# Gated linear attention with an MLP on one core: first two batches loaded one by one, exp(-L) first in chunk 0, constants in two loads, and a new sequence of turns

## The chip, the core and the metric

The kernel runs on one core of a Trainium2 chip. The metric is the device time of one execution in microseconds (us). Before the change three executions took 438.69, 439.83 and 440.66 us; the median is 439.83 us. The profile was taken in a further execution of 438.57 us, whose span (first to last instruction) is 436.8 us; the 1.8 us between the two lie around the span.

## What is computed

```python
def _attn_ref(q, k, v, alpha):            # each (4, 8, 768, 48): batch, head, step, dim
    state = zeros((B, H, D, D))
    for t in range(S):
        state = alpha[:, :, t, :, None] * state + einsum('bhd,bhe->bhde', k[:, :, t], v[:, :, t])
        y[:, :, t] = einsum('bhd,bhde->bhe', q[:, :, t], state)

def _moe_ref(x, g_ln, w_ch1, w_ch2):      # x: (4, 768, 384), the heads of y side by side
    xn = (x - mean(x)) / sqrt(var(x) + 1e-06) * g_ln
    return x + maximum(xn @ w_ch1, 0.0) @ w_ch2      # w_ch1 (384, 1536), w_ch2 (1536, 384)
```

The weights arrive as 64-bit floats, which the kernel reads as pairs of 32-bit words and turns into 32-bit floats itself.

## The kernel before

**Tiles and stages.** The 768 steps are cut into 6 chunks of 128, and each of the 4 batches goes through each chunk, so there are 24 attention blocks. A block (`attention(c, b)`) does the following:

- ScalarE takes the logarithm of alpha (line 278, tile `la`); TensorE sums it over the steps with a triangular matrix (line 284 in chunk 0, line 288 later, tile `lps`, in PSUM). The sum is called L.
- ScalarE computes exp(L) into the SBUF tile `eq` (line 291) and exp(-L) back into the PSUM tile `lps` (line 292).
- VectorE multiplies k by exp(-L) (line 294) and q by exp(L) (line 296) into the tile `qk`.
- One row of `eq` goes to DRAM (line 301, tile `row`) and comes back as columns (line 361, tile `gate`): the decay of the state over the block.
- TensorE transposes `qk` (line 321, tile `tps`), and ScalarE and VectorE copy the result to SBUF (`qT` line 328, `kT` line 326). TensorE multiplies the two (line 337 in chunk 0, line 345 later, tile `aps`), and VectorE copies the causal half (lines 350 and 355, tile `at`).
- TensorE computes the update of the state (line 371, tile `ups`); VectorE multiplies it by the gate in chunk 0 (line 380), and later adds it to the state (line 384), after which GpSimd multiplies by the gate (line 386). TensorE computes the output (line 397 in chunk 0, line 407 later, tile `yps`).
- ScalarE and VectorE normalize the output (lines 414 to 440, tile `xn`), and TensorE transposes it (line 446, tile `xps`) into `xT`.

The MLP of chunk 0 is a plain product (line 476, tile `hps`, and line 488). From chunk 1 on both products are split into blocks that are combined with fewer multiplications (lines 765 and 588), with sums before and after on VectorE, ScalarE and GpSimd.

**Weights.** Twelve pieces of 768 KB are loaded (line 192, tile `ws`, three buffers) and rounded by five VectorE instructions (lines 204, 206, 208, 212, 214) with one of ScalarE (line 210) between the third and the fourth.

**What sets the order.** Every stage is a Python generator that issues some instructions and yields. The string `ORDER` is a list of turns: each letter names a generator, and a letter runs it to its next yield. `a` to `x` are the attention blocks (`a` to `d` are the batches of chunk 0), `A` to `L` the weight pieces, `Y` and `Z` the first product of chunk 0, `M` and `V` the later products, and so on. So `ORDER` fixes the order of the instructions in every engine's queue, SyncE's queue of transfers too. Each queue runs in order, and an instruction that waits holds up all behind it.

**Start.** ScalarE issues the load of the constants (triangle, identity and a second mask: 160 KB, line 163) and of `g_ln` (line 176). SyncE issues four loads of alpha of chunk 0, one for each batch (192 KB each), and then, as the turns come, k and q of two batches at a time (384 KB each, line 128) and v (line 134). Transfers share eight semaphores in turn, so the ninth waits until the first has landed, the tenth until the second, and so on. TensorE runs eight matmuls on zeros (line 231) while the first data come in.

Of the kernel before, what the change touches and what calls it, by code (L numbers as in the profile page):

```python
# [9 lines left out]
FP32 = mybir.dt.float32  # L10
# [3 lines left out]
AFT = mybir.ActivationFunctionType  # L14
# [8 lines left out]


ORDER = (
    "aaaabbaaddaacbbbbccccaaababbbccdddaaabbbbfeaAfffeeeadaaebbfdaaddceadcccceeeehAdd"
    "gdAccaachbeAgbfbbffffghddddbcggghccibceeeaggghaeebbifffggfBdddddfjcifggeeecAeeCB"
    "hccefiifhhhhcBBYYYdjhiffcjcdYiiYjjZffZiiYYDjDCBDflCCZZZDkYZZZlhhlihhgiiigjjjilYY"
    "gjgghEYYlGEZZGZhEZYlmkhkjggjghllYYYCkkkGEZhlFFHkkiiiYOOFFFlYYenZZZmlhjjYfHHggDjj"
    "GlmjjkeZZZZYhhhSJZYnkkkleekkkkiOlZnkiemmllYZZiinmmmnnfmmYIeIfholHPPSSomjjSSSkSSm"  # L30
    "KIIkkjKKpjJJnnknQfflQoojLLngggmLWWWQPPSPPSSPPpoSoEnhmmgghhnXQXXOXppQppiiiXXQQSSS"
    "mmmnliOjjXXXSmmlnniijMSoWWWoMMrXMMXooMMMMMMmnnnMMMMMRMMmMmMMqMppMMMMMppWMqolorrp"
    "lpppQjjpRRRMMMMMMMpprppMqqqrLnooqqppqqWWWoMMMMRmrMtRMoMMMMRMMMMMMMnnnMMOMMOssqqO"
    "tqsqskMoRooqqtttqWWRNNNMMMMMRRqtNMNNNnnnnNMMMMMMMMMMMlllMkkkMMMkRNNlNNMMNBtvmWtt"
    "pMMNtrllmMMMMrkkrNNMMMMMMMMMossXXXMMtrvvrrrqqqrrXXXooXMMMMMMMXXMMMoXMXrooMMMMMoM"
    "MsMIMMMMsMrMvssvMMMMvtruuustMssrrrtsssuqmMttMMMMRMMMMtMMtuurrrrMMrMppMMMMMMMqROR"
    "MRRRMMMMRRROMpMMMpNOONNNnMMnMMMMRRRNMMMMMNNNMNMMwNMNMMMMMMMMMMMNNNvvMNNvppovxMoM"
    "MMMmMsMMMxqqqvtAXXsssXXvvvXMXvXvttMuMMMMMXXsXuMMMMMMMMMMMuMMMMRMMOtuXMMxMMMMttMM"
    "MMwwwwuquusvuuMMMMMwwwwMMMxuRMMRRRxMMMMMwMRMMRMMMMMMxxxxMMMOOxRMwswwwvRwxuxNNswx"
    "xxNNKquMMMvvttsuuxMMsMMMtRRNNNMMMRMMMxqNNxNwxrrMMMCMMMNMMMONMMNssMMMNMMMMMMvvvww"  # L40
    "vNNMMMwwtXXXXxXxxXMLuuXXMMMXXMMMMMMMMMMMMMMMMMMwMOuMMwxOxxMMvXuuwMMRMMMMMMMMMMMw"
    "JJMMwMMMMMMRRRMMMMMuMRMMMMMvxRRRMMMRMMMMXXXXVXXXOMMXXXRMMRNMMMMMVVNNVVVVVVVNXNMV"
    "VVVRVVVVVMVVVVVVVVVVNRRMNNVVVVVVVVVVVVMRRRRMMMMMVVVVONNNNNMMMMMMNVRVVVVVMMMMMMVV"
    "VRRVVVVRNRNVVOMMNNMMMNGNNMMMMMMNNMMOOKMMMMMMMMMMMNNNRMMMMMMNNNOMMMMHNMMNMMMMMNMM"
    "MMMMMMMM"
)

# [2 lines left out]
def kernel(  # L50
# [51 lines left out]
    raw = ctx.enter_context(tc.tile_pool(name="raw", bufs=B // 2))  # L102
# [10 lines left out]
    r = np.arange(P)  # L113
    const_np = np.concatenate([np.triu(np.ones((P, P), np.float32)), np.eye(P, dtype=np.float32),
                               np.tile(np.triu(np.ones((HS, HS), np.float32)), (2, 1))], 1)

    raws = {}

    def load(c, m, names):

        bs = range(2 * m, 2 * m + 2)
        rows = slice(c * P, (c + 1) * P)
        for n, src in (("a", alpha), ("k", k), ("q", q)):
            if n in names:
                t = raw.tile([P, 2, 2, NP, D], FP32, name=f"r{n}", tag="in", bufs=6)
                step = 1 if n == "a" and c == 0 else 2
                for i in range(0, 2, step):
                    nc.sync.dma_start(
                        t[:, i:i + step].rearrange("t b i p d -> t b (i p d)"),
                        src[bs.start + i:bs.start + i + step, rows].rearrange("b t h d -> t b (h d)"))  # L130
                raws.update({(n, c, b): t[:, b - bs.start] for b in bs})
        if "v" in names:
            vn = raw.tile([P, 2, 2, NP, D], FP32, name="vn", tag="vn")
# [3 lines left out]
            if c:  # L137
# [3 lines left out]
                src = v[bs.start:bs.stop, rows].rearrange(  # L141
                    "b (s t) (i p) d -> s i t b (p d)", s=2, i=2)
# [3 lines left out]
            for b in bs:  # L146
                raws["v", c, b] = vn[:, b - bs.start], vx[:, b - bs.start] if c else None

    lone = {}

    def load_one(n):
# [8 lines left out]
                              rows.rearrange("t h d -> t (h d)"))  # L160

    consts = cpool.tile([P, 2 * P + HS], FP32, name="consts")
    nc.scalar.dma_start(consts, nc.inline_tensor(const_np, name="consts").ap())
    tri, ident = consts[:, :P], consts[:, P:2 * P]
    mask, mask_of_halves = tri.bitcast(INT32), consts[:, 2 * P:].bitcast(INT32)
    for m in range(B // 2):
        load(0, m, "a")

    w1 = cpool.tile([P, NJ // 2, NF, 2 * P], FP32, name="w1")
    w2 = cpool.tile([P, NJ, DM], FP32, name="w2")  # L170
# [94 lines left out]
    def attention(c, b):  # L265


        whole, last = c == 0, c + 1 == NCB
        if whole and b % 2 == 0:
            load(0, b // 2, "kq")  # L270
            yield
            load(0, b // 2, "v")
            yield

        qk = qk_of(c, b).rearrange("t n p i c -> t n i p c")[:, :, :, :, :D]
        eq = eq_of(c, b).rearrange("t p i c -> t i p c")[:, :, :, :D]
# [17 lines left out]
        nc.vector.tensor_mul(qk[:, 1], raws.pop(("k", c, b)), lv)  # L294
        yield
        nc.vector.tensor_mul(qk[:, 0], raws.pop(("q", c, b)), eq)  # L296
        ends = slice(P - 1, P) if whole else slice(HS - 1, P, HS)
# [581 lines left out]
```

## Time and profile before

| | |
|---|---|
| median of three executions | 439.83 us (438.69 to 440.66) |
| profiled execution | 438.57 us, span 436.8 us |
| TensorE (PE) busy | 425.2 us, 4760 matmuls |
| VectorE (DVE) busy | 340.0 us, 654 instructions |
| ScalarE (ACT) busy | 202.4 us |
| GpSimd (POOL) busy | 156.0 us |
| granted TensorE clock | full in all slices |
| moved by DMA | 45.53 MB |

In the profile a line such as "L294 DVE TENSOR_TENSOR qk<-rk,lps" is the instruction of line 294 on VectorE that writes tile `qk` from tiles `rk` and `lps`; the brackets behind a row give the idle time of the engine before it and what ended it. PEld is TensorE's loading of weights, which runs beside its matmuls; SPq and ACTq are issues of transfers. Matmuls on 32-bit data show as two rows each, transposes as one. The busy time of TensorE is modelled, so short waits can hide in it; the time between the starts of matmuls shows them.

The trace also records when the last packet of each transfer landed. For the loads at the start these are, in us from the start of the span:

| transfer | KB | issued | landed |
|---|---|---|---|
| alpha, batch 0 | 192 | 0.73 | 3.86 |
| constants | 160 | 0.76 | 4.06 |
| alpha, batch 1 | 192 | 1.19 | 4.54 |
| g_ln | 1.5 | 1.17 | 4.73 |
| alpha, batch 2 | 192 | 1.65 | 5.94 |
| alpha, batch 3 | 192 | 2.12 | 7.68 |
| k, batches 0 and 1 | 384 | 2.59 | 8.73 |
| q, batches 0 and 1 | 384 | 3.07 | 9.77 |
| v, batches 0 and 1 | 384 | 3.87 | 10.83 |
| k, batches 2 and 3 | 384 | 6.28 | 11.85 |
| q, batches 2 and 3 | 384 | 6.71 | 12.89 |

Each transfer is spread over 16 DMA engines. From alpha of batch 3 on, one of the 16 finishes about 1.05 us behind the other fifteen (6.63 against 7.68 us for that transfer): a single packet of it took 1.34 us at 4.59 us, where most take 0.065 us.

### The profile page before, as it was taken

To read this page: it belongs to the slowest core of one execution; us is meant where nothing else is said; L and a number is where in the kernel's file an instruction comes from. 1 tells how busy PE (TensorE), PEld (TensorE's weight loads), DVE (VectorE), ACT (ScalarE), POOL (GpSimd) and SP (SyncE) were. 2 spreads that over 40 slices of the span, in tenths; PEclk is the share of its full clock that TensorE was granted. 3 is DMA by queue.
4 is the path that set the end of the run, shared out by engine and by line. 5 is a ranking of instruction groups with operands and counts; after the bars stand their busy time and mean duration, and the time that the engine had idled before them with its cause. 6 is when DMAs were issued, how large, how long until landed. Compare 5 with 4: busy or idle time off the path is not lost.

```text
span 436.8 us, 11605 instructions
## 1 busy us (share of the span) xinstructions
PE 425.2 (97%) x4760; PEld 379.5 (87%) x4760; DVE 340.0 (78%) x654; ACT 202.4 (46%) x499; POOL 156.0 (36%) x164
## 2 busy tenths in 40 slices
PE   6998999999999999999999999999999999999996
PEld 4887888875678889998789998889998899999996
DVE  3997999898898889957769756678685589786682
ACT  4795656554534546734285141655246442402000
POOL 1011041310015556042854133672026472638213
PEclk9999999999999999999999999999999999999999
DMA  8989877755162085022351013310033000001201
GB/s 271 333 197 331 257 228 222 201 146 147 45 175 72 22 220 165 1 93 74 58 151 50 18 39 126 59 21 2 2 110 108 2 1 2 0 0 56 78 32 55
DMA packets 54973, 45.53 MB, mean 104 GB/s; under 512 B 26204, under 2 KB 51036, under 8 KB 54920
## 3 DMA queue, kind: packets, MB, share of 16 engines
q1 hardware_dynamic: 54376, 44.63, 34.9%
q8 instruction: 37, 0.61, 0.6%
q10 hardware_dynamic: 544, 0.17, 0.2%
q14 instruction: 16, 0.13, 0.1%
HBM read 35.25 MB, written 9.53 MB: 103 GB/s over the span
## 4 chain that ended last, share of the span: by engine, by line
PE 80%; DVE 8%; DMA 6%; ACT 2%; issue 1%; POOL 1%; SPq 1%; POOLq 0%; ACTq 0%
PE ops L588 29%; PE hps L765 29%; PE ops L488 5%; PE yps L407 4%; PE aps L345 3%; PE tps L321 3%; DMA rq<-in_q_dram 3%; PE xps L446 2%; PE ups L371 2%; PE hps L476 2%; DVE w L206 1%; DMA vn<-in_v_dram 1%; DMA gate<-row 1%; DVE ws L212 1%; PE lps L288 1%
## 5 line engine op out<-in xcount | busy, mean ns | idle before, releaser
L604 POOL TENSOR_TENSOR ob<-ob,u 128x192 f32<-128x192 f32 x40 | 24.9, 632 | 81.9 <-DVE ob L601 57.8
L765 PE MATMUL hps<-sum,w 128*128 128x256 f32 x192 | 47.2, 379 | 0.0
L386 POOL TENSOR_TENSOR mid<-mid,gate 112x192 f32<-112x192 f32 x20 | 17.6, 880 | 70.8 <-DVE mid L384 60.0
L765 PEld LDWEIGHTS hps<-sum,w 128*128 128x128 f32 x192 | 35.9, 190 | 4.6
L588 PE MATMUL ops<-w,hT 128*128 128x192 f32 x224 | 39.6, 326 | 0.0
L816 ACT ACTIVATE hT<-hT 128x512 f32<-128x512 f32 x48 | 28.1, 631 | 21.6 <-POOL hT L787 13.2
L588 PEld LDWEIGHTS ops<-w,hT 128*128 128x128 f32 x224 | 37.0, 190 | 0.4
L765 PE MATMUL hps<-xT,w 128*128 128x256 f32 x136 | 34.6, 381 | 0.0
L476 PE MATMUL hps<-xT,w 128*128 128x256 f32 x144 | 32.6, 379 | 1.8 <-DVE qk L294 1.8
L488 PE MATMUL ops<-w,hT 128*128 128x384 f32 x96 | 31.7, 487 | 0.0
L476 PEld LDWEIGHTS hps<-xT,w 128*128 128x128 f32 x144 | 26.7, 190 | 5.3 <-issue 2.0
L598 DVE TENSOR_TENSOR ob<-ops,ob 128x192 f32<-128x192 f32 x50 | 17.1, 351 | 15.9 <-POOL ob L604 8.8
L588 PE MATMUL ops<-ws,sum 128*128 128x192 f32 x160 | 28.8, 326 | 0.0
L488 PEld LDWEIGHTS ops<-w,hT 128*128 128x128 f32 x96 | 17.9, 190 | 11.8 <-ACT qT L328 0.2
L765 PEld LDWEIGHTS hps<-xT,w 128*128 128x128 f32 x136 | 25.3, 190 | 3.3
L588 PEld LDWEIGHTS ops<-ws,sum 128*128 128x128 f32 x160 | 26.3, 190 | 0.0
L386 POOL TENSOR_TENSOR st<-st,gate 112x192 f32<-112x192 f32 x16 | 12.6, 786 | 35.5 <-DVE st L384 35.5
L321 PE MATMUL tps<-consts,qk 128*112 128x128 f32 x176 | 24.2, 275 | 0.0
L588 PE MATMUL ops<-ws,hT 128*128 128x192 f32 x128 | 23.4, 326 | 0.0
L345 PE MATMUL aps<-qT,kT 48*64 48x64 f32 x640 | 23.1, 222 | 0.0
L321 PEld LDWEIGHTS tps<-consts,qk 128*112 128x112 f32 x176 | 19.9, 134 | 3.0 <-DVE qk L296 0.6
L407 PE MATMUL yps<-st,qT 48*64 48x48 f32 x320 | 22.3, 219 | 0.0
(230 smaller groups left out, 1159.3 us busy)
## 6 DMA issues: line engine op xcount, KB each, us to landing
ws<-in_moe_w_ch_dram SPq DMA_DIRECT2D x12, 768.0 KB
vn<-in_v_dram SPq DMA_DIRECT2D x12, 384.0 KB
kept<-x SPq DMA_DIRECT2D x24, 192.0 KB
ob<-kept SPq DMA_DIRECT2D x24, 192.0 KB
out_dram<-ob SPq DMA_DIRECT2D x19, 192.0 KB
ra<-in_alpha_dram SPq DMA_DIRECT2D x16, 192.0 KB
rk<-in_k_dram SPq DMA_DIRECT2D x6, 384.0 KB
rq<-in_q_dram SPq DMA_DIRECT2D x6, 384.0 KB
```

The costliest lines, as they stand in the source:

```text
L321: nc.tensor.transpose(tps[:, p], qk_of(c, b)[:, i, p].rearrange("p a b -> p (a b)")[:, :R], ident)
L345: nc.tensor.matmul(aps[0][halves[1 - i], p, s], kT[rs, p, s], qT[rs, p, s], start=True, stop=True)
L371: nc.tensor.matmul(up[h, p], qk_of(c, b)[ts, 1, p, i, :h.stop - h.start], vn[ts, i, p], start=True, stop=True)
L386: nc.gpsimd.tensor_mul(new, new, by)
L407: nc.tensor.matmul(yps[r][halves[s], i, p], of, by, start=True, stop=True)
L476: nc.tensor.matmul(hps, w1[:, j // 2, f, j % 2 * P:][:, :P], xT_of[0][:, f, bs], start=(f == 0), stop=(f == NF - 1))
L488: nc.tensor.matmul(ops_of[b], hT_of[c][:, j, b], w2[:, j], start=(j == 0), stop=(j == NJ - 1))
L588: nc.tensor.matmul(acc, lhs[:, j], rhs[:, j], start=(j == 0), stop=(j == NT - 1))
L598: nc.vector.tensor_add(x, acc, x)
L604: getattr(nc.gpsimd, f"tensor_{op}")(x, x, y)
L765: nc.tensor.matmul(acc[:, i], w, b, start=True, stop=True)
L816: nc.scalar.activation(out=x, in_=x, func=AFT.Relu)
```

## The change

The loads of chunk 0 for batches 0 and 1 become six transfers of 192 KB in the order alpha, k, q of batch 0, then alpha, k, q of batch 1 (`load_first`). Alpha, k and q of batches 2 and 3 are loaded together, 384 KB each, in the first turn of batch 2, as later chunks do. In chunk 0 ScalarE computes exp(-L) before exp(L), and writes it into the SBUF tile `la` (the logarithms, which are no longer needed) where it wrote to PSUM before. The constants come in two loads: the triangle (64 KB) first, and the identity with the second mask (96 KB) behind `g_ln`. The string `ORDER` is new throughout; its first lines are shown. The number of compute instructions on each engine is unchanged; SyncE and ScalarE issue one transfer more each.

```diff
-    "aaaabbaaddaacbbbbccccaaababbbccdddaaabbbbfeaAfffeeeadaaebbfdaaddceadcccceeeehAdd"
-    "gdAccaachbeAgbfbbffffghddddbcggghccibceeeaggghaeebbifffggfBdddddfjcifggeeecAeeCB"
+    "acaaaaaabbbbbbccaaadaaccbbccddbbdfdaaabeeeffbbaebbbcBdbfaAefccccddddadBgddcccbbb"
+    "ghabbBffBeeeeecccgaaaacchfbggAffddhhddfafgffdffCgabiAAjgggjjeaiiffeeggfhhceieecc"
...
-                step = 1 if n == "a" and c == 0 else 2
-                for i in range(0, 2, step):
-                    nc.sync.dma_start(
-                        t[:, i:i + step].rearrange("t b i p d -> t b (i p d)"),
-                        src[bs.start + i:bs.start + i + step, rows].rearrange("b t h d -> t b (h d)"))
+                nc.sync.dma_start(t.rearrange("t b i p d -> t b (i p d)"),
+                                  src[bs.start:bs.stop, rows].rearrange("b t h d -> t b (h d)"))
...
+    def load_first():
+
+        ts = [(n, src, raw.tile([P, 2, 2, NP, D], FP32, name=f"r{n}", tag="in", bufs=6))
+              for n, src in (("a", alpha), ("k", k), ("q", q))]
+        for b in range(2):
+            for n, src, t in ts:
+                raws[n, 0, b] = t[:, b]
+                nc.sync.dma_start(t[:, b].rearrange("t i p d -> t (i p d)"),
+                                  src[b, :P].rearrange("t h d -> t (h d)"))
...
-    nc.scalar.dma_start(consts, nc.inline_tensor(const_np, name="consts").ap())
+    const_src = nc.inline_tensor(const_np, name="consts").ap()
+    nc.scalar.dma_start(consts[:, :P], const_src[:, :P])
...
-    for m in range(B // 2):
-        load(0, m, "a")
+    load_first()
...
         nc.scalar.dma_start(g_col, g_ln.rearrange("(f p) -> p f", p=P))
+    nc.scalar.dma_start(consts[:, P:], const_src[:, P:])
...
         if whole and b % 2 == 0:
-            load(0, b // 2, "kq")
+            if b:
+                load(0, b // 2, "akq")
...
-        nc.scalar.activation(out=eq, in_=lv, func=AFT.Exp)
-        nc.scalar.activation(out=lv, in_=lv, func=AFT.Exp, scale=-1.0)
+
+        by = la if whole else lv
+        for out, sign in ((eq, 1.0), (by, -1.0))[::-1 if whole else 1]:
+            nc.scalar.activation(out=out, in_=lv, func=AFT.Exp, scale=sign)
         yield
-        nc.vector.tensor_mul(qk[:, 1], raws.pop(("k", c, b)), lv)
+        nc.vector.tensor_mul(qk[:, 1], raws.pop(("k", c, b)), by)
```

More of the change, by code (lines that the diff above doesn't have):

```diff
@@ L25 @@
 ORDER = (
-    "aaaabbaaddaacbbbbccccaaababbbccdddaaabbbbfeaAfffeeeadaaebbfdaaddceadcccceeeehAdd"
-    "gdAccaachbeAgbfbbffffghddddbcggghccibceeeaggghaeebbifffggfBdddddfjcifggeeecAeeCB"
[L28 to L43, printed above, removed]
@@ L44 @@
-    "VRRVVVVRNRNVVOMMNNMMMNGNNMMMMMMNNMMOOKMMMMMMMMMMMNNNRMMMMMMNNNOMMMMHNMMNMMMMMNMM"
+    "acaaaaaabbbbbbccaaadaaccbbccddbbdfdaaabeeeffbbaebbbcBdbfaAefccccddddadBgddcccbbb"
+    "ghabbBffBeeeeecccgaaaacchfbggAffddhhddfafgffdffCgabiAAjgggjjeaiiffeeggfhhceieecc"
+    "cgYffhhhihYddCYeYckjceeedAjiegggkhhhhdCeCBiikiiYddhhffYYDDZZlYYgZZZZhhlEDiiYiiii"
+    "ggEEjjelYYYYYYEHZllCDllHFlZZZkhjiiHihFjjGZggFhFiileeZmlGkhnZYYmllZnGGjCjlOelHelI"
+    "YYmImOOmYYjYYjJkkkkkZZmmmIIKjJhJJKLLmmPPKKPPLPWePooOhjjkknkiiiiiggggkknjmjnoomIW"
@@ new lines @@
+    "mSSnngnnngjjOPhPhhhkQlfSSSSSWWSSZZkkSQQgjjmmppnnkffmmmOfpplnlppZZZZZSfXXXXZXkkkS"
+    "SSSSpopppQQlXXXXXXGmWmnnWlQQWnnMMMMMMoqllQMMmMMllWMMMMMMMMSMqqpppppqqnnpqoooMMMM"
+    "OnMMrrpooooroooiiMMMrRWWllMMMMMMMMMMrMRRRRMMMnnMMMMMMnRnnrtRqqqqMMMWMMMRMMkMRotq"
+    "qMpmoooDpNNlNNRRNloMMMWWMMMNonmMjjMMMMMpkkNNNqMRMNkNNMrrOppMMrMNrMMsMMsrrqkpmmMM"
+    "MMMMomtkNNNppMqMssqMMXjjpjMXFqXXttMMMOMXXXMMrrtrqqrqqsvsMntttrMMMMMMMrrvXXtXXtts"
+    "sMvMMMvuMssMrrOOMMMMMMMMMMMMMMMMRRuRRsssttttMssmvMMMMMMuMMMMMMMMMMMMMMuMMMquMMML"
@@ new lines @@
+    "MmoovMnRRMMttRRRMMMNNNNMMMOttpMMRRMNNNNMMtMMMMMMLqrNNRNoMMNMMMqqquNxvvMMMMMNvNwM"
+    "MMsssvMMMMMuMMMpNrrssswwvvvvvwwooXsXuuMuXwXXXXXMMMMMxuuuvvxuxXXMMMMMMMMMvvMxtMMM"
+    "MMMMXMMMMMMMMMMttMMusRRRMMMRMMMsMMMxxRtRMMOOMMMxxMMruwMMwwwMMMxMMtMMMuuuwwuvRRww"
+    "wrxxxxxxqssMMMsARNRMMMsRONNNxuuNNwwNNNwOrMMMMrRMMMMMvMMMMMMuwNNxttNNMMMMMMMMqXXX"
+    "XNXXXMMMwNMNMMMMMuXXXXMMuMMMMMMMMMMMMMwwwMMMMMOOwMxxRMMMxHMMMMMMMMMMxxvRRMMMMMvv"
+    "MxMMMMMMwRMMMMxMMwMMMMMuxvvRRRREMMMRMMRMRNNNNMMNMMXVXXXXXXVMNMMNMMOMMXXXXMMMMRVV"
@@ L45 @@
+    "VVVVNNNVVVVVVVVVMVVNMMMVMMOMMMNVVOVVVVVVVVVVVVRRVVNVVVVJVBVVVVVVVVMMMRRRMRMNNMOV"
+    "VVVVNMMMMMMMRRVVVVVVMMMMMKORMNNMMONNMMMRRMNNMMMRNNNMMMMMNNNMMMMMMNMMNMMMMMMNNMMM"
     "MMMMMMMM"
```

## The prediction

> **What bounds the kernel now.** The first part of the page gives busy time by engine:
>
> ```profile
> PE 425.2 (97%) x4760; PEld 379.5 (87%) x4760; DVE 340.0 (78%) x654; ACT 202.4 (46%) x499; POOL 156.0 (36%) x164
> ```
>
> TensorE's work doesn't change, so only its idle time can be won. I take it from the time between the starts of matmuls: where each kind's steady pace (in us: 0.109 a transpose, 0.125 L337, 0.063 L397, 0.432 L476 and L765, 0.326 L588) is exceeded, TensorE waits. From the first real matmul on this adds up to 13.7 us: 2.9 before 10.4 us, 2.6 from there to 37.1, 1.95 in one gap there, and 6.2 after 39.3, scattered. Behind the last matmul come some 4 us of sums and stores. So the page's busy time hides waits; a table of stretches (us busy, with counts) shows who is full in the head:
>
> ```profile
> core 0: us, PE busy (x) PEld busy (x) DVE busy (x) ACT busy (x) POOL busy (x), PEclk, DMA share, GB/s
> 4.50:10.40 5.90, 3.38 (x10) 1.14 (x8) 1.16 (x3) 3.11 (x7) 0.00 (x0) 1.00 1.02 348
> 10.40:20.00 9.60, 9.59 (x162) 8.14 (x163) 8.92 (x18) 6.35 (x15) 0.00 (x0) 1.00 1.01 320
> 20.00:30.00 10.00, 10.00 (x225) 8.83 (x223) 9.73 (x17) 9.46 (x28) 1.44 (x2) 1.00 0.93 273
> ```
>
> VectorE does almost nothing before 10.4 us and is then full; the DMA engines are full from the start. The timeline says what VectorE waits for, and how closely its work follows afterwards:
>
> ```profile
> 8.86 0.55 DVE L294 TENSOR_TENSOR qk<-rk,lps 128x384 f32<-128x384 f32 x1 [6.19 <-DMA rk<-in_k_dram]
> 9.79 0.56 DVE L296 TENSOR_TENSOR qk<-rq,eq 128x384 f32<-128x384 f32 x1 [0.38 <-DMA rq<-in_q_dram]
> 10.27 0.55 DVE L294 TENSOR_TENSOR qk<-rk,lps 128x384 f32<-128x384 f32 x1
> 10.73 0.55 DVE L296 TENSOR_TENSOR qk<-rq,eq 128x384 f32<-128x384 f32 x1
> ```
>
> It waits 6.19 us for k, then one product follows the other every 0.47 us. So the head is first DMA-bound, then VectorE-bound, to about 37 us. The table of waits for 26 to 40 us names the next two:
>
> ```profile
> POOL mid L386 <- DMA gate<-row: 2.4, 1, 2.4
> PEld hps L476 <- issue: 2.0, 1, 2.0
> ```
>
> GpSimd waits for a gate column to land (32.8 us). The gap of 1.95 us in TensorE's stream at 37.1 us (inside the first MLP products, L476) has no releaser: "issue". The page's DMA part explains it:
>
> ```profile
> q8 instruction: 37, 0.61, 0.6%
> ```
>
> 37 packets of 16 KB for 2 x 4760 TensorE instructions make one block of 256 instructions each. One such packet ran from 36.75 to 37.94 us, and the gap ended 1.3 us later. The gaps at 54.1 (0.44), 83.5 (0.56) and 215.0 us (1.26) lie at the same place modulo 256 instructions (within 10). So where TensorE runs through a block of small matmuls faster than the next block comes, it stands still.
>
> **The change, part by part.**
>
> *Loads.* The sixteen engines share one stream, so I place the new transfers by bytes in the table of landings: alpha, k and q of batch 0 land at 3.86, 4.54 and 5.94 us, alpha of batch 1 (now fourth) at 7.68, k and q of batch 1 by 8.7, alpha, k and q of batches 2 and 3 at 9.8, 10.8 and 11.85, v at 12.9. The triangle (64 KB of the 160) is there when the whole was, 4.06, or sooner. The extra issues (0.4 to 0.5 us each on SyncE and ScalarE) lie ahead of waits that end last anyway: ScalarE's next instruction waits for alpha until 3.88 us.
>
> *The chain of chunk 0.* L278 at 3.88, matmul at 4.51, its result at 5.40 as now. exp(-L) comes first: ready 5.88, so k of batch 0 is multiplied at 5.9 instead of 8.86. But in TensorE's new queue the sum of batch 1 stands ahead of the transposes of batch 0, and it needs the fourth transfer: logarithm 7.70 to 8.22, matmul 8.27, result 9.16 (0.89 as for batch 0), exp(-L) to 9.65, k of batch 1 at 9.7, q at 10.2. Then ScalarE's queue decides: exp(L) 9.55, the logarithm of batch 2 at 10.0, qT 10.4, the logarithm of batch 3 at 10.9, exp(-L) of batch 2 from 11.4 to 11.9. VectorE: k 11.9, q 12.4, kT 12.9, k 13.5, q 14.0, so the first L350 starts at 14.45 instead of 14.93: **0.5 us earlier**. If the one lagging DMA engine does not lag (alpha at 6.63, the rest 1.05 us earlier) the same steps give 13.35: 1.6 us. So an early start of 3 us shrinks to 0.5 to 1.6.
>
> *exp(-L) into SBUF.* ScalarE's median is 491 ns into SBUF (L291) and 486 into PSUM (L292); VectorE takes 547 ns with the PSUM operand (L294), 552 without (L296). Nothing either way. The Trainium skill ("ScalarE: Activation LUTs", Step-by-step: what each stage is for) says that PSUM is the faster destination for ScalarE, which speaks against this edit; the rows show 5 ns, and four of them would be 0.02 us.
>
> *The sequence.* From L350 on VectorE's queue is nearly the old one for 13 us of work. Then the new sequence puts the first three instructions of the second weight piece (0.58 + 0.99 + 0.48 = 2.05 us, L204, L206, L208) ahead of the L436 that makes `xn` of batch 1, for which TensorE waits (L446). TensorE has almost the same work before that point: 24.3 us instead of 24.7 (four transposes of 0.109 fewer). Before, the two rows stand so:
>
> ```profile
> 30.28 0.47 DVE L436 TENSOR_SCALAR xn<-x,few 128x384 f32<-128x384 f32 x1
> 31.23 0.49 PE L446 MATMUL xps<-consts,xn 128*128 128x128 f32 x3
> ```
>
> After: 30.75 + 2.05 less 0.5 to 1.6 is 31.2 to 32.3, so TensorE has idled 0.5 to 1.5 us more there than before. Second limit: the load of the second weight piece (768 KB, at 1.05 us for 384 KB about 2.1 us) now stands in SyncE's queue ahead of the gate that landed at 32.77:
>
> ```profile
> 32.90 0.51 POOL L386 TENSOR_TENSOR mid<-mid,gate 112x192 f32<-112x192 f32 x1 [2.44 <-DMA gate<-row]
> ```
>
> It lands at 34.9 at worst, GpSimd is done by 35.4, and the L407 that reads the product comes after 27.7 us of TensorE work: 35.5 - 1.05 (its start) - 27.7 = 6.7 us idle, against 5.0 before at that kind of place (33.97 us, 28.0 of work). With DMA gaps taken up (share 0.93), less. I take **+1.2 us** for this stretch (bounds +0.5 and +1.6).
>
> *Instruction blocks.* Counted along the new queue, the block that cost 1.95 us (4.7 us of TensorE work to cover its load) becomes two blocks of 4.0 and 4.45 us. At that time a block took 3.3 us from request to packet, 1.2 to move and 1.1 to act. Against that TensorE now waits for VectorE and the gate part of the time. I take 1.35 us (bounds 0.5 and 2.3): **-0.6**. Later, the old queue has four blocks with 2.0 to 2.6 us of work, and the gaps of 0.56 and 1.26 fall on two of them; the new one has one of 2.8, the rest 3.9 or more. I take **-1.3** (bounds 0 and -2.2). The Trainium skill ("Runtime: NRT & Kernel Launch", Instruction fetch mechanics) states blocks of 16 KiB, 256 instructions, and calls crossing a boundary mostly hidden. The block size agrees with the 37 packets; the trace's 1.95 us is not hidden. By the page both terms would be nothing, and the sum +1.6.
>
> *VectorE's lead later.* Between 60 and 100 us of TensorE work, VectorE's work up to the results that TensorE waits for was 6 to 8 us less than TensorE's own; now it is 2.1 to 3.4 less. VectorE was by then 12 to 15 us behind its count, mostly waiting on others. What cover is left I can't see: **+0.4** (bounds 0 and +1.5).
>
> *The end* is unchanged: the last eleven VectorE and GpSimd instructions stand in the same order.
>
> **Sum:** +1.2 - 0.6 - 1.3 + 0.4 = -0.3 us: 438.57 becomes 438.3. The median shown lies 1.26 above the profiled execution, so 439.5 against 439.83. What a measurement tells from no change is about 0.5%, 2.2 us.
>
> **Rivals.**
>
> 1. *As summed* (no change that can be told): the earlier start is used up by the second weight piece. 439.5; its own bounds add up to -3.15 and +3.45, and 437.6 to 442.0 is its range. This holds the case that the change doesn't do what it says, because TensorE's transposes of batch 0 stand behind batch 1's sum: the first L350 stays at 14.9, and 0.5 is added.
> 2. *Faster:* no DMA engine lags, VectorE gains 1.6 us, and the blocks of instructions come in time: +0.5 - 1.45 - 2.2 + 0.2 = -2.95, so 436.9. For: the four short blocks are gone. Against: the lag came from one packet of 1.34 us among first accesses, and the new order has as many first accesses.
> 3. *Slower, by the late gate:* the place is GpSimd's first L386. From 34.1 us on (VectorE's own limit) each us that the gate lands later is a us of TensorE. For: DMA share 0.93 to 1.0 in this time, 768 KB put ahead. Against: the column is small, and DMA had gaps after 28 us. To lose 2.2 us in all, with the other terms as summed, it must land about 36.6; with VectorE's next sums queued behind it the price is then some 2.5 us: 442.3.
>
> **How the numbers follow.** Chances: as summed 0.45, faster 0.32, slower 0.23; the same stand for within 0.5%, faster and slower. The predicted time is 439.5. The range takes in rival 2 with a bit beyond its sum (436.0) and rival 3 (442.8); outside lie the bounds met all at once.
>
> **What would show it.** First VectorE L294 at 5.9, first L350 at 13.3 to 14.5; the L446 of batch 1 at 31.2 to 32.4; first L386 of GpSimd at 34 to 35.5, waiting for the gate; the first L476 after 29.3 us of work, near 37 (before 36.0 after 29.8); a gap "issue" there of 0.5 to 2.3 us; afterwards gaps at block boundaries of less than 1 us in sum, where there were 2.3. It is wrong if VectorE starts L350 before 13, if the L446 is not late, or if the idle time after 60 us, where I only counted queues, differs by more than 2 us.

## The result, and the profile after

The changed kernel takes 445.91 us (median of 4 runs, 444.87 to 448.08) beside 440.25 for the kernel before: a ratio of 1.0153, 95% interval 1.0107 to 1.0199. Forecast were 439.5 and a range of 436.0 to 442.8, so it is slower than the whole range. A second measurement, beside other experiments (new_again below, 10 runs of 440.0 to 445.56), gave 1.0085 (1.0056 to 1.0114). It is slower in both, by an amount that differs from run to run.

The profiled execution took 448.08 us with a span of 446.3, the slowest of the four. First the page of the kernel after, its part 1 and the row of the granted clock in 40 slices:

```profile
PE 432.0 (97%) x4760; PEld 381.9 (86%) x4760; DVE 341.4 (77%) x654; ACT 203.4 (46%) x499; POOL 153.7 (34%) x164
...
PEclk9999998999999999999999999999999999999999
```

TensorE's busy time rose by 6.8 us at the same 4760 matmuls. Part of that is clock: the seventh slice (67 to 78 us) is below 9. The table of stretches of the kernel after, with the columns of before:

```profile
core 0: us, PE busy (x) PEld busy (x) DVE busy (x) ACT busy (x) POOL busy (x), PEclk, DMA share, GB/s
4.50:10.40 5.90, 4.03 (x16) 2.12 (x16) 2.55 (x5) 3.33 (x8) 0.00 (x0) 1.00 0.96 314
10.40:20.00 9.60, 8.74 (x127) 6.84 (x126) 7.70 (x16) 5.99 (x15) 0.00 (x0) 1.00 1.00 330
20.00:30.00 10.00, 10.00 (x178) 8.05 (x176) 9.86 (x18) 8.47 (x24) 0.95 (x1) 1.00 1.00 305
...
40.00:45.00 5.00, 2.38 (x10) 2.07 (x10) 3.79 (x9) 2.04 (x6) 1.00 (x2) 0.84 1.05 305
70.00:74.00 4.00, 1.55 (x83) 1.37 (x76) 3.02 (x4) 1.37 (x2) 0.22 (x1) 1.00 0.58 176
74.00:78.00 4.00, 4.00 (x16) 3.29 (x15) 2.25 (x4) 3.20 (x10) 0.00 (x0) 0.57 0.66 231
```

VectorE starts sooner (5 instructions by 10.4 us, before 3), as planned. The new sights are two stretches in which TensorE stands still, 40 to 45 and 70 to 74 us, and a lower granted clock that begins behind each standstill (0.84 in the first stretch, 0.57 from 74 to 78 us). The table of waits names what released TensorE in them (who waits, for what; us in total, times, the longest):

```profile
PE tps L332 <- issue: 2.7, 1, 2.7
...
PE yps L418 <- issue: 2.4, 1, 2.4
```

Nothing: "issue", as for the gap at 37 us before the change. Between the starts of the matmuls, less a steady step, these two gaps are 2.87 us (from 39.6) and 2.56 us (from 70.8); gaps below are given so. The single instructions answer to those shown of before (the timeline of the kernel after: start, duration, and in brackets the idle time ahead and what ended it; L305, L361, L447, L457 and L397 are the old L294, L350, L436, L446 and L386):

```profile
6.59 0.56 DVE L305 TENSOR_TENSOR qk<-rk,la 128x384 f32<-128x384 f32 x1 [3.92 <-ACT la L303]
...
14.21 1.93 DVE L361 COPY_PREDICATED at<-consts,aps 128x512 f32<-128x512 int32 x3
...
30.81 1.38 DVE L216 TENSOR_SCALAR ws<-ws 128x768 int32<-128x768 int32 x1
...
30.83 0.95 POOL L431 MEMSET at<- 128x1024 f32 x1 [2.29 <-PE yps L408]
...
32.84 0.47 DVE L447 TENSOR_SCALAR xn<-x,few 128x384 f32<-128x384 f32 x1
...
33.45 0.52 PE L457 MATMUL xps<-consts,xn 128*128 128x128 f32 x3 [0.65 <-DVE xn L447]
...
34.27 0.51 POOL L397 TENSOR_TENSOR mid<-mid,gate 112x192 f32<-112x192 f32 x1 [2.49 <-DVE mid L395]
```

The head gains 0.7 us by 14.2 (forecast 0.5 to 1.6) and loses it by 33: `xn` of batch 1 is 2.6 us later than before, and TensorE now waits for it.

Where the time went, by TensorE's time over its steady pace (idle, and lost to a slow clock), in us of each stretch:

| kernel | 0 to 10 | 10 to 35 | 35 to 60 | 60 to 100 | after | sum |
|---|---|---|---|---|---|---|
| before, profiled at 438.57 | 3.0 | 2.6 | 2.5 | 1.5 | 4.1 | 13.7 |
| after, profiled at 448.08 | 3.2 | 5.0 | 4.5 | 5.4 | 4.2 | 22.3 |
| the same (new_again), profiled at 440.00 | 2.9 | 5.4 | 1.6 | 0.9 | 3.4 | 14.1 |

Two profiles of one program: a loss of 2.4 and 2.8 us more than before between 10 and 35 us is in both, the rest is in one only. The sums are short by some 1 us for the changed kernel: they exceed that of before by 8.6 and 0.4 us, the spans by 9.5 and 1.4.

### The profile page after: what moved, and what is told of

It is laid out like the page before. It is cut to its first block, busy times and chain, and to the rows that moved or that the text cites. A ratio compares the mean times of both kernels' runs of the same rounds, so it can differ in the third digit from the quotient of the medians.

```text
span 446.3 us, 11603 instructions
## 1 busy us (share of the span) xinstructions
PE 432.0 (97%) x4760; PEld 381.9 (86%) x4760; DVE 341.4 (77%) x654; ACT 203.4 (46%) x499; POOL 153.7 (34%) x164
## 4 chain that ended last, share of the span: by engine, by line
PE 82%; DVE 8%; issue 3%; DMA 2%; ACT 2%; POOL 1%; POOLq 0%; SPq 0%; DVEq 0%
PE ops L599 28%; PE hps L776 26%; PE ops L499 7%; PE hps L487 5%; PE yps L418 4%; PE tps L332 3%; PE aps L356 3%; PE xps L457 2%; PE ups L382 2%; DMA ra<-in_alpha_dram 1%; DMA rq<-in_q_dram 1%; DVE w L214 1%; PE lps L239 1%; PE lps L297 1%; DVE more L559 1%
## 5 line engine op out<-in xcount | busy, mean ns | idle before, releaser
L615 POOL TENSOR_TENSOR ob<-ob,u 128x192 f32<-128x192 f32 x40 | 26.6, 674 | 83.6 <-DVE ob L612 61.4
L397 POOL TENSOR_TENSOR mid<-mid,gate 112x192 f32<-112x192 f32 x20 | 14.1, 710 | 64.7 <-DVE mid L395 39.2
L487 PE MATMUL hps<-xT,w 128*128 128x256 f32 x144 | 35.8, 400 | 0.1
L776 PE MATMUL hps<-xT,w 128*128 128x256 f32 x136 | 34.3, 379 | 0.0
L487 PEld LDWEIGHTS hps<-xT,w 128*128 128x128 f32 x144 | 27.8, 200 | 4.4 <-DVE qk L305 0.5
L776 PEld LDWEIGHTS hps<-xT,w 128*128 128x128 f32 x136 | 25.5, 190 | 3.2
L332 PE MATMUL tps<-consts,qk 128*112 128x128 f32 x176 | 25.6, 279 | 0.0
L795 POOL TENSOR_TENSOR hT<-hT,u 128x512 f32<-128x512 f32 x8 | 10.4, 1296 | 43.9 <-DVE u L794 43.9
L418 PEld LDWEIGHTS yps<-st,qT 48*64 48x64 f32 x320 | 20.6, 135 | 5.1 <-issue 4.2
```

Source lines behind the costliest of these rows:

```text
L332: nc.tensor.transpose(tps[:, p], qk_of(c, b)[:, i, p].rearrange("p a b -> p (a b)")[:, :R], ident)
L397: nc.gpsimd.tensor_mul(new, new, by)
L418: nc.tensor.matmul(yps[r][halves[s], i, p], of, by, start=True, stop=True)
L487: nc.tensor.matmul(hps, w1[:, j // 2, f, j % 2 * P:][:, :P], xT_of[0][:, f, bs], start=(f == 0), stop=(f == NF - 1))
L615: getattr(nc.gpsimd, f"tensor_{op}")(x, x, y)
L776: nc.tensor.matmul(acc[:, i], w, b, start=True, stop=True)
```

## The experiments

Theories, by the letters used in the expectations. **A**: TensorE's code comes in blocks of 256 instructions; the fetch of a block queues behind bulk loads, TensorE stalls, and the stall slows the clock. **B**: the new sequence's order on VectorE. **C**: the edits of code in the head. **D** came later: the clock in the first 10 us. Lags below are from where TensorE's count crosses into a block to the start of the next fetch packet; records are missing here and there, so a lag is good to about 1 us. The end of a stall needs no such count: in the nineteen profiles the starts of two matmuls in a row lie over 1 us apart 37 times after 20 us, and 31 of these gaps end 1.2 to 1.6 us after the end of a fetch packet (before the change 37.94 and 39.28 us; after it 41.20 and 42.62, 72.06 and 73.42). The waits table names VectorE, ScalarE or GpSimd for the other six.

### The two halves of the change apart: new_code_old_order, old_code_new_order

The first has the code of after with the old ORDER (its first `c` moved from place 12 to 1):

```
-    "acaaaaaabbbbbbccaaadaaccbb...
+    "acaaabbaaddaabbbbccccaaaba...
```

> The changed kernel's code (loads batch by batch, exp(-L) first and into SBUF, constants in two loads) under the old sequence of turns; one turn, the first of the third attention step, had to move from place 12 to place 1, because the code now issues that step's alpha load there. Theory A (TensorE's instruction blocks are fetched behind bulk loads, and where a block boundary meets a full queue is set by the sequence): the boundaries stand against the loads as before the change, so 440 us, within 1.5 of the kernel before, at a granted clock of 1.0, with no wait without releaser above 2.3 us. Theory B (the new sequence's order on VectorE, the second weight piece ahead of xn of batch 1, costs the time): also about 440. Theory C (the edits of code in the head cost it): 444 to 446, as the changed kernel.

Measured: 443.72 us, ratio 1.0108 (1.0076 to 1.0139). All three missed. In the profile (441.71, the shortest of four) the whole loss lies before 16 us: the first attention product (the old L337) starts at 15.14 us, before 12.37, and from there to 334 us the two run 2.7 to 3.1 us apart. Part of it is the clock, granted at half from 11.44 to 14.85 us: the sixteen transposes that took 2.02 us before the change take 3.40.

```profile
11.81 3.40 PE L332 MATMUL tps<-consts,qk 128*112 128x128 f32 x16
```

```profile
11.40:14.90 3.50, 3.50 (x17) 3.13 (x16) 0.69 (x1) 1.73 (x4) 0.00 (x0) 0.51 0.89 285
```

The second has the code of before with the ORDER of after.

> The code of before (alpha loaded for all batches at the start, exp(L) first, one load of constants) under the new sequence of turns. Theories A and B (the sequence alone): 443 to 447 us, with two waits of TensorE without releaser of over 2 us, near 40 and near 71 us. Theory C (the edits of code): 439 to 441.5, as before.

Measured: 446.88 us, 1.0186 (1.0161 to 1.0211), with gaps of 2.19 us at 42.0, 2.08 at 48.3 and 1.52 at 72.9. The two stretches are as A has them, but the head loses again: first attention product at 15.43, with the clock at half from 8.19 to 15.02 us. So the halves can't be told apart by crossing them: each crossing costs about 3 us in the head, by waits and by a slow clock after them. That each sequence fits the order in which its own code's loads land is likely, but not shown.

### The blocks moved: new_shift128, old_shift160

```
+    def tiny(n):
+        for _ in range(n):
+            nc.tensor.matmul(idle[:32, :1], zero[:, :32], zero[:, :1], start=True, stop=True)
-    for _ in range(8):
+    for _ in range(6):
         nc.tensor.matmul(idle[:, :P], zero, zero, start=True, stop=True)
+    tiny(10)
...
             nc.tensor.matmul(lps[:, :DM], tri, a, start=True, stop=True)
+            if b == 0:
+                tiny(24)
```

> The changed kernel with 128 more TensorE instructions at its start (32 more matmuls of the warm-up, tiny ones of 32 rows by 1 column; 6 instead of 8 full ones), so that every later boundary between blocks of 256 instructions falls 128 instructions earlier in the work; the rest of the program is the same. Theory A: the waits of 2.87 us at 39.6 and 2.56 us at 70.8 go, and the halved clock after each of them, unless new ones come where the shifted boundaries lie close together (near 32 and near 47 us, 4.3 and 4.8 us for a block): 439 to 442 us at a granted clock of 1.0. Theory B or C: 444 to 447, whatever happens to the two waits, since the time lost would then be lost again at the next wait for VectorE. The tiny matmuls themselves may cost up to 1 us at the start.

Measured: 442.83 us, 1.0101 (1.0083 to 1.0119), the profiled run 441.0. The median lies between the two forecasts. Both big stalls are gone; gaps of 1.38 at 37.3 and 0.94 at 44.5 remain. Since in another run of the unaltered kernel they are 0.97 us and nothing (new_again, below), this profile alone doesn't show that the stall follows the count of instructions; the next kernel does.

old_shift160 does the same to the kernel before (12 and 30 tiny ones).

> The kernel before the change with 160 more TensorE instructions at its start (40 more matmuls in the warm-up, tiny ones, 6 full instead of 8), nothing else. Theory A: the boundaries move away from the full stretch of the queue, the wait of 1.95 us at 37 falls to at most 0.6 and that of 1.17 us at 215 goes, so 0.5 to 2.5 us faster than the kernel before, or even with it if the tiny matmuls cost 1 us in the first 10 us. If where the boundaries fall does not matter: the same time as before within 0.5 us plus the cost of the tiny matmuls, the wait at 37 unchanged.

Measured: 443.34 us, 1.0077 (1.0046 to 1.0108), but unevenly spread: three runs at 439.6 to 439.9, seven at 442.6 to 443.9. In the profile (439.88) the gaps at 37 and 215 are gone and new ones of 1.5 at 128.9 and 1.09 at 258.9 are there, where two boundaries now lie 1.8 and 1.9 us apart. The gap near 37 us stands in all six profiles with the old order and boundaries unmoved or nearly so (1.7 to 3.6 us) and in none of the three with moved ones (this kernel, old_fill_shift160, old_fill_shift128): it follows the count of instructions, not the work. The three shorter runs show a mean clock of 0.995 to 0.996, the seven longer ones 0.998 to 1.0; a late start of the full clock would do that (old_order_edits, below), but none of the longer runs was profiled.

### Fewer loads ahead of the fetch: new_split_load, new_late_load

```
             load_one(n - 1)
-            load_one(n)
...
             next(turns[turn], None)
+            if i == 286:
+                load_one(3 * B + 1)
```

> The changed kernel with three of the six 192 KB loads that were issued between 63.3 and 65.9 us (chunk 3, batch 1) put behind the next weight load, at about 71.5 us; nothing else differs. Theory A: the transfers ahead of the block's fetch shrink by 0.58 MB, about 1.6 us of the queue, so the wait of 2.56 us at 70.8 falls to about 1, no halved clock follows it, and the kernel is 2 to 4 us faster than the changed one: 441 to 444. Theory B or C: 444 to 447, no gain.

Measured: 444.81 us, 1.0132 (1.0112 to 1.0153). The wait at 70.9 is 1.51 us instead of 2.56, and no halved clock follows; the one at 40.3 is 2.74. In time no gain is shown (1.0132 against 1.0153 and 1.0085), and since the unaltered kernel has a run with no wait at this place (new_again), the shorter wait proves nothing by itself.

new_late_load moves one `C` of ORDER from place 127 to behind 152.

> The changed kernel with one turn moved: the load of 768 KB that was issued at 32.5 us goes behind the three loads of the next chunk, to about 36.7 us, which is after the point (35.75) where TensorE's queue crosses into a new block. Nothing else differs. Theory A: 0.77 MB, about 2.1 us of transfers, no longer stand ahead of the block's fetch, so the wait of 2.87 us at 39.6 falls to about 1, no halved clock follows it, and the kernel is 1.5 to 3 us faster than the changed one: 442 to 444 on the scale of a kernel before at 440. If the fetch were late for another reason than the loads ahead of it: the wait stays at 2.5 to 3 us and the time at 444 to 446.

Measured: 445.39 us, 1.0157 (1.0103 to 1.0211): no gain. In the profile the stall near 40 did go (0.2 us of "issue" is left in that stretch), but there are gaps of 1.61 us at 48.8 and 2.05 at 74: the moved load may now stand in the way of the next fetch. The profiled run is the longest of four (449.14; the others 444.52 to 445.86): TensorE waited 1.9 us for VectorE's `kT` at 21.6, and the clock was at half from 23.61 to 30.43 us.

### The second weight piece later: new_shift128_late_piece

The kernel is new_shift128; in its ORDER the three `A` at 109, 132, 133 go behind 130, 131, 146.

> As new_shift128, and the second weight piece's three VectorE instructions (2.0 to 3.0 us before xn of batch 1) put behind the xT of that stage, its other two behind the sums of the next state; all before the first hidden product needs the piece. Theory B (the new sequence's VectorE order costs the 2.2 us that TensorE idles more than before the change between 10 and 35 us): xn of batch 1 comes 2 us sooner, TensorE's wait of 0.8 us at 32 goes, and the kernel is 1 to 2.5 us faster than new_shift128. Theory A alone (only the blocks count): within 0.7 us of new_shift128, since the same VectorE work is then late for the next thing.

Measured: 445.21 us, 1.0134 (1.0100 to 1.0169), slower than new_shift128. `xn` is in time, but the piece's ScalarE instruction now stood ahead of a logarithm. Waits and timeline of this kernel:

```profile
PE lps L305 <- ACT la L293: 3.6, 1, 3.6
```

```profile
37.29 0.97 ACT L218 ACTIVATE ws<-ws,small 128x768 int32<-128x768 int32 x1 [3.51 <-DVE ws L216]
38.16 0.51 ACT L293 ACTIVATE la<-ra 128x384 f32<-128x384 f32 x1
```

ScalarE waits 3.51 us for VectorE's L216 with the logarithm queued behind, and TensorE for that. The experiment added a wait and doesn't decide on B; a better placed one follows below.

### The edits without the new sequence: old_order_edits

The diff is the change's, without ORDER, and with alpha of the other two batches still loaded at the start:

```
-    for m in range(B // 2):
-        load(0, m, "a")
+    load_first()
+    load(0, 1, "a")
```

> The kernel before the change, its sequence untouched, with the three edits of the head: the first two batches loaded batch by batch (alpha of the other two behind them, still at the start), exp(-L) first and into SBUF, constants in two loads. new_code_old_order lost 2.8 us in the first 15 us, and there one turn had been moved to place 1. If the edits themselves lose it under the old sequence (its TensorE order asks for the third and fourth batches' alpha early, which now comes later): 2 to 3.5 us slower than before. If the moved turn lost it: within 1 us of before, the first product of VectorE 0.5 us or so sooner.

Measured: 442.82 us, 1.0076 (1.0044 to 1.0108), 3.4 us over the kernel before beside it: the edits lose it without the moved turn. The timeline of TensorE, here and before the change:

```profile
9.22 2.93 PE L294 MATMUL lps<-la,consts 128*128 128x384 f32 x4 [0.35 <-ACT la L288]
11.95 2.92 PE L332 MATMUL tps<-consts,qk 128*112 128x128 f32 x16
```

```profile
9.47 0.91 PE L284 MATMUL lps<-la,consts 128*128 128x384 f32 x2 [0.28 <-ACT la L278]
10.41 2.02 PE L321 MATMUL tps<-consts,qk 128*112 128x128 f32 x16
```

The same transposes start every 0.21 us instead of 0.109: TensorE ran at half speed until 14 us. The table of stretches calls the clock 1.00 there, and the run's mean is 1.0, since the clock's record only begins with the first window at full speed (14.0 us in this run, 4.4 before, 5.8 after). So "clock 1.0" doesn't say that the head was fast. Here the first attention product starts at 14.80 us, 2.4 later than before; the gap near 40 us, 2.4 us against 1.95 at 37, is another part.

### The head kept busy: new_fill, new_fill_shift128, old_fill, old_fill_shift160

All keep the 8 warm-up matmuls and add work on zeros in TensorE's idle stretch near 6 us; "fill" in few big instructions, "shift" in many small ones.

```
+            if b == 0:
+                for _ in range(2):
+                    nc.tensor.matmul(idle[:, :3 * P], zero, wide, start=True, stop=True)
```

```
+            if b == 0:
+                for _ in range(32):
+                    nc.tensor.matmul(idle[:32, :32], zero[:, :32], zero[:, :32], start=True, stop=True)
```

> The changed kernel with two matmuls of 128x128 by 384 on zeros (their result is read by nobody) behind the first cumulative sum, in the 1.7 us that TensorE idles at 5.9; 8 instructions, so the block boundaries stay nearly where they are. Theory D, formed after the last runs (batch-by-batch loads leave TensorE too idle in the first 10 us, so that in some runs, by the phase of the 3.41 us windows in which the clock is granted, the clock comes to full speed late; in old_order_edits the matmuls ran at half speed until 14 us): 1 to 2.5 us faster than the changed kernel at the median, 442.5 to 444.5 on the scale of 440 before, while the two waits of over 2 us at 40 and 71 stay. Theory A alone (blocks, whatever the head's clock): no gain, 444.5 to 446.5.

Measured: 443.44 us, 1.0121 (1.0094 to 1.0147). That lies between the two measurements of the changed kernel, so a gain by D is not shown here. Gaps of 2.15 at 40.3 and 1.65 at 47.

> The changed kernel, its 8 warm-up matmuls kept, with 32 matmuls of 32x32 by 32 on zeros (128 instructions, 31 ns a pass in new_shift128, about 2 us) in the same idle stretch. Theories A and D together: no wait over 1.5 us after 20 us, and the clock kept in the head: 439.5 to 442, faster than new_fill by 2 to 4 us. Theory D alone: as new_fill. Theory A alone: as new_shift128 in its slower runs, 443 to 444.

Measured: 441.29 us, 1.0066 (1.0043 to 1.0090), range 440.86 to 441.77, 2.15 us faster than new_fill beside it, as A and D together have it. It stays 2.8 us slower than before the change: two waits of about 1.5 us are left, for GpSimd at 37.3 and at a block boundary at 49.1, and the loss between 10 and 35 us.

> The kernel before with three such 128x128 by 384 matmuls behind the second cumulative sum, in its idle stretch of 2.3 us at 5.9: the control for the filling. Theory D: the runs of the kernel before that show a mean clock of 0.996 take 1.5 to 2 us more than the others; with the gap filled these go, so the median is 0 to 1.5 us lower, with less scatter. Otherwise: the same within 0.5.

(Three matmuls, behind the sum of batch 1.) Measured: 441.30 us, 1.0068 (1.0044 to 1.0093): slower, against both expectations. The waits and the stretches of old_fill:

```profile
PE hps L481 <- DVE qk L299: 3.4, 1, 3.4
```

```profile
30.00:35.00 5.00, 5.00 (x179) 4.77 (x177) 4.42 (x10) 4.10 (x13) 1.24 (x3) 1.00 0.79 159
35.00:40.00 5.00, 1.58 (x8) 1.15 (x6) 4.54 (x10) 3.22 (x8) 0.79 (x2) 0.83 1.10 340
40.00:45.00 5.00, 5.00 (x97) 4.25 (x97) 1.58 (x2) 0.38 (x1) 0.00 (x0) 0.83 1.05 391
```

The head was 0.8 us faster (first attention product at 11.51 us). TensorE came to the block boundary at 35.2 instead of 37.1, the block's packet came at 36.26 to 37.26 instead of 36.75 to 37.94, and the stall grew from 1.95 to 3.58. All four runs have a mean clock of 0.995. The releaser in the table is not to be trusted: VectorE's `qk` at 38.29 was merely the last event before TensorE went on. In old_shift160 the same products run from 38.12 and that VectorE instruction comes at 40.63, after them.

> The kernel before, 8 warm-up matmuls kept, with 40 matmuls of 32x32 by 32 (160 instructions, about 2.5 us) in the same idle stretch. Theory A: the waits of 1.95 us at 37 and 1.17 us at 215 go, as in old_shift160, against new ones of 1.5 at 129 and 1.1 at 259; with the head's clock kept 436.5 to 438.5, faster than both kernels. If the gain of the shift is given back by the new waits: 438.5 to 440.5.

(40 small ones.) Measured: 439.77 us, 1.0030 (1.0016 to 1.0044), so the second case: given back at 127.8 (1.51 us) and 257.4 (1.30).

### Boundaries where nothing is tight: old_fill_shift128

32 small ones instead of 40.

> As old_fill_shift160, with 32 small matmuls instead of 40 (128 instructions): the pairs of boundaries that lie 1.8 and 1.9 us apart there, where TensorE stalled 1.5 us at 128 and 1.3 us at 257, come to lie 3.3 and 2.8 us apart, and the full stretch near 30 to 34 us has two boundaries 3.9 us apart. Theory A: stalls of 1.5 and 1.3 go, one of at most 1 us comes near 34: 437 to 438.7, faster than old_fill_shift160 by 1 to 2 and as fast as the kernel before or faster. If the position of the boundaries is not what counts: the same as old_fill_shift160, 439.5 to 440.3.

Measured: **436.40 us** (9 runs, 434.63 to 437.67), ratio 0.9930 (0.9907 to 0.9953): faster than both kernels and than the forecast, though it does more work than either. Its stretches, to compare with old_fill:

```profile
30.00:35.00 5.00, 4.64 (x142) 4.27 (x145) 4.17 (x11) 3.78 (x12) 0.91 (x2) 1.00 0.53 85
35.00:40.00 5.00, 5.00 (x89) 4.42 (x83) 4.00 (x11) 3.57 (x11) 1.02 (x2) 1.00 1.08 336
40.00:45.00 5.00, 4.29 (x110) 3.86 (x102) 4.97 (x10) 3.15 (x7) 0.51 (x1) 1.00 1.06 390
```

old_fill and this kernel fill the same idle stretch and run the same work behind it. They differ in 116 instructions of count, and by 1.4% in time, each against the kernel before beside it.

### A load that nobody reads: old_spare_load, old_spare_load_early

```
+            if i == 351:
+                spare = dram.tile([P, B, DM], FP32, name="spare", tag="spare", bufs=1)
+                nc.sync.dma_start(spare, alpha[:, :P].rearrange("b t h d -> t b (h d)"))
```

> The kernel before the change with one more transfer that nobody reads, 768 KB of alpha copied to spare memory, issued at about 80.2 us, just before TensorE's queue crosses into a block at 81.1 and the next 2.2 us later; there the fetch began 0.42 us after the crossing and TensorE stalled 0.47 us at 83.5. Theory A (the fetch stands in the queues behind the bulk transfers issued before it): the fetch begins 2 to 4 us after the crossing, TensorE stalls 1.5 to 4 us at 83 to 87 with no releaser of its own, and the kernel takes 1.5 to 5 us more. If blocks are fetched past the bulk transfers: the fetch stays within 1 us of the crossing, the stall at about 0.5, and the time within 0.7 of the kernel before.

Measured: 438.94 us, 1.0004 (0.9978 to 1.0029). The load was issued at 81.4, too late for the fetch meant; the next fetch's lag rose from 1.77 to 3.95 us, and its block was not needed for 11 us. A late fetch that nobody waits for cost nothing.

> As old_spare_load, the transfer issued 3 us sooner, at about 78.2 us. In old_spare_load it came too late for the fetch that was meant (0.41 us after its crossing) and hit the next one, whose lag went from 1.77 to 3.95 us, but the block after that was not needed for 11 us, so nothing stalled. Here 768 KB stand in the queues when TensorE crosses at about 80.3 to 81.1, with the next boundary 2.2 us later. Theory A: fetch 2 to 4 us after the crossing, a stall of 1.5 to 3.5 us near 83 that the kernel before has at 0.47, and 1 to 4 us more in all. If a fetch passes bulk transfers that nobody waits for: lag and stall as before, time within 0.7 us.

(`i == 333`.) Measured: 443.34 us, 1.0107 (1.0079 to 1.0136). The load was issued at 78.3 us. The lag is 1.77 us instead of 0.42, a little under the forecast. The wait there, in this kernel and in the kernel before:

```profile
PE ups L371 <- issue: 1.5, 1, 1.5
```

```profile
PE ups L371 <- issue: 0.4, 1, 0.4
```

A transfer on whose data nothing depends makes TensorE stall 1.1 us more. This is no scatter: in the five other such profiles of the old order (before, old_spare_load, old_fill, new_code_old_order, old_order_edits) the step between matmuls there is 0.50 to 0.61 us, here 1.69. That bulk loads delay the fetch is shown by cause. The 4.4 us in all are more than this stall explains; the profile is of the shortest run (440.22), the three others have a mean clock of 0.990 to 0.992. In the profile GpSimd also starts on the gate behind the load 1.8 us later than before (85.78 against 84.00). How these share the rest stays open.

### The second weight piece again: new_fill_shift128_late2

In new_fill_shift128's ORDER the `A` of 109, 132, 133 go behind 130, 139, 146.

> As new_fill_shift128, and the second weight piece's three VectorE instructions behind the xT of that stage, its ScalarE instruction behind the two exps of the next step (in new_shift128_late_piece it had stood ahead of a Ln and TensorE waited 3.6 us for that Ln), its last two VectorE instructions behind the next state's sum. TensorE idles 2.4 us more than before the change between 10 and 35 us. Theory B (that is the order on VectorE, the piece ahead of xn of batch 1): the waits for xn and kT near 21 and 33 us shrink by 0.8 to 2 us in sum, and the kernel is 0.8 to 2 us faster than new_fill_shift128, 439.3 to 440.5. Rival (the lead that VectorE and ScalarE lose is only moved): within 0.5 of new_fill_shift128, with a new wait at 35 to 48 us in its place.

Measured: 444.11 us, 1.0095 (1.0064 to 1.0127), between 440.49 and 446.34. In the profile (440.49, the shortest of ten), 10 to 35 us loses about 1 us less than in new_fill_shift128 (4.2 against 5.1, counted as in the table above). Then the waits of 33 to 45 us:

```profile
PE hps L490 <- DVE w L222: 1.4, 1, 1.4
PE yps L421 <- POOL mid L400: 1.4, 1, 1.4
```

TensorE waits for the weight piece itself, and as in new_fill_shift128 for GpSimd. The rival is right in kind, with new waits in the old one's place; the time is worse than it said, 4.7 us over the kernel before beside it where new_fill_shift128 was 2.8. In this profile VectorE has no lead in this stretch, and what is put last is waited for. Theory B in its simple form, one piece in the wrong place, falls.

### The changed kernel again: new_again

> The changed kernel itself, unaltered, to tell its own scatter beside the runs that start from it: 444 to 448, ratio to the kernel before 1.012 to 1.018. Theories A and D: in runs with a mean clock of 1.0 still 443.5 to 445, since stalls without a halved clock after them remain; two halved windows after the stalls add up to 3.4.

Measured: 443.55 us, 1.0085 (1.0056 to 1.0114), so below the expected ratio. Five of the ten runs have a mean clock of 0.999 or 1.0 and took 440.0 to 444.73; three of them are under the forecast for such runs. Its profiled run (440.00) has no halved clock after the start. Waits and stretches, to set beside those of the first profile:

```profile
PE tps L332 <- issue: 0.8, 1, 0.8
```

```profile
40.00:45.00 5.00, 4.19 (x123) 3.69 (x124) 4.93 (x11) 3.21 (x9) 1.39 (x2) 1.00 1.06 303
67.00:71.00 4.00, 4.00 (x102) 3.68 (x95) 3.93 (x7) 3.53 (x9) 0.27 (x1) 1.00 0.63 180
```

The first stall is under 1 us, the second is not there. The same fetch and the same loads meet in both runs. Here the packet of the second ran from 62.98 to 63.91 us, ahead of the second weight load's data (landing 64.67 to 66.61) and six more loads. In the first profile the same loads stood 3 us later, the weights landed from 67.47 and the six loads by 71.74, and the packet ran from 71.09 to 72.06. Whether the packet or the loads come first decides over 2.5 us of stall. Why the order differed isn't shown: in both runs the first of the two weight loads was issued 4.9 us before TensorE's count crossed into the block.

## Why the prediction was wrong

- **Loads and the chain of chunk 0: the result right, in part by luck.** First L350 forecast 13.35 to 14.45, measured 14.21. But the lag of one DMA engine, from which 14.45 came, was not there for alpha of batch 1 (landed 6.56 us; 7.68 forecast with the lag, 6.63 without), and without it the forecast was 13.35. Two other delays came instead: the first product of k came at 6.59 instead of 5.9, since the first sum took 1.40 us (the next one 0.91; the full clock is on record from 5.82 us), and q of batches 2 and 3 landed at 12.10 instead of 10.8 (without the lag).
- **exp(-L) into SBUF:** no effect, as forecast (0.49 us for one in chunk 0, 0.48 into PSUM before).
- **The sequence, +1.2 (bounds 0.5 and 1.6): right in mechanism, too small.** Measured +2.4 and +2.8; `xn` reached TensorE at 33.45 (forecast 31.2 to 32.4), and the first L476 ran at 38.0 (forecast near 37). From the first L350 to `xn` of batch 1 VectorE took 18.6 us, before 15.4. Of the 3.3 more, 2.05 was forecast; 0.82 is L216, which took 1.38 us instead of 0.56 while a GpSimd MEMSET ran (lines above; 1.38 in new_again too), and 0.5 is a longer wait for ScalarE at 17.5. The late gate (rival 3) was not it: GpSimd at 34.27 waited for VectorE.
- **Instruction blocks, -0.6 and -1.3: the step that failed.** I sized a stall as the shortage of TensorE work in a block, against one fetch time taken from one gap. The runs show a fetch lag of 0.4 to 0.9 us in quiet queues and 3.5 to 4.6 (good to 1 us) behind bulk loads. For one block, with the same loads ahead of it, it was some 4.6 us in the first profile of the changed kernel and about nothing in the second. So the stalls were 2.87 and 2.56 in the first profile, 0.97 and nothing in the second. From 35 us on, the stretches of the second sum to -2.2 against before, near my -1.9, or to some -1.2 if the 1 us that the table misses lies there; those of the first sum to +6.0. The term was a race with an open end of some +3, and I gave it a bound of +0.35. My sign of being wrong, idle time after 60 us off by more than 2 us, came in the first profile (+4.0 against before, where my terms gave -0.9).
- **What was missing: the clock.** Each stall of the first profile was followed by a window of 3.41 us at half clock (43.37 to 46.78 and 74.09 to 77.50). TensorE can lose up to 1.7 us in each, and the prediction has no term for it. A halved clock after the head isn't needed for a time above the forecast: of the fourteen runs of the changed kernel six have a mean clock of 0.999 or 1.0, and they took 440.0 to 444.87 us (median 443.5); the eight others have a median of 445.3.
- **VectorE's lead later, +0.4:** not seen. The second profile is 0.6 us under before between 60 and 100 us and 0.7 after.
- **The end:** unchanged, as forecast.

The Trainium skill ("DMA: Bandwidth & Descriptors", Queues, rings and completion order) says that each DMA engine goes round the queues that have work, one packet at a time. By that a fetch would wait for a packet, not for all the loads issued before it. The section counts 9 to 17 descriptors to a packet as typical and 64 as the most, so one wait could itself be 0.6 to 1.1 us and up to 4.2 (an estimate, with 0.065 us for a row of this trace taken as one descriptor). The spare load raised two lags by 1.35 and 2.18 us (0.42 to 1.77 and 1.77 to 3.95), more than the one and less than the other, so it doesn't decide; when a request was sent no run here shows.

What stays open: which of these makes up the typical run of the changed kernel, some 4 us over before, since only its slowest and its fastest run were profiled. If the sequence costs 2.4 to 2.8 us in it too, 1.3 to 1.7 of the 4.1 in new_again are left (an estimate) where the blocks and the lead were to give -1.5.

## What to carry to other kernels

Where a fully unrolled program runs through small matmuls while loads fill the queues, look up the instruction fetch packets in the trace and see how long a block lasts there; a change of the sequence moves every later boundary, and a faster head can make the stall longer (old_fill). Before trusting a few tenths of a per cent for an edit, move the boundaries by a hundred idle instructions and measure again: old_fill and old_fill_shift128 differ in little else, and stand at +0.7% and -0.7%. Give a term that is a race the whole width of the race.

## What the runs showed of the hardware

- The halved clock comes on a fixed grid of 3.413 us: the two slow windows of the first profile begin 30.72 us apart, nine times that. What counts is the idle time within one such window: with 2.65 and 2.6 us in the window before, the clock was halved, and in new_late_load with 2.0 (a gap from 21.6 us in the window of 20.19 to 23.61); the gap of 2.74 us in new_split_load, cut by the grid at 42.3 us into 1.9 and 0.8, left it full, and so did 1.96 us in one window of old_code_new_order (from 42.32). So in these runs the limit lies near 2 of the 3.41 us, an estimate from these gaps. The Trainium skill ("TensorE: Matmul & The Clock Gate", What's actually happening) calls this window free-running, and the grid agrees; its advice to avoid gaps over some 3 us (Why this matters for your kernels) is too mild for the gaps of 2.87 and 2.56 us in the first profile and of some 2.0 us in new_late_load.
- The grid's phase differs from run to run, so TensorE first comes to full speed anywhere from 4.1 to 14 us in the profiles here (the changed kernel at 5.8 in one, 4.7 in the other), and the mean clock of a run leaves that time out. In five profiles the clock then fell back to half for one or two windows between 7.6 and 15 us.
- Matmuls of 32x32 by 1 or 32 start every 31 to 32 ns at full clock, so 32 of them (64 passes) took 2.0 us (5.11 to 7.12 in new_fill_shift128).
- A VectorE TENSOR_SCALAR on 128x768 (int32) took 1.38 us instead of 0.56 while a GpSimd MEMSET of 0.95 us ran, 1.06 and 0.76 where it met only the last 0.64 and 0.34 us of one (new_fill, new_shift128). A SCALAR_TENSOR_TENSOR of the same size beside such a MEMSET took its usual 0.96.
